# All key-value products of an attention, MLP and expert kernel made early and parked in DRAM, and the last chunk's routing drawn into three steps

## Chip, cores and metric

One Trainium2 chip, one of its cores. The metric is the device time of one execution in microseconds (us). Three runs of the kernel before gave a median of 1302.85 us (1300.02 to 1303.67).

## What is computed

Three stages follow each other on 4608 tokens (8 batches of 576), with 512 features each.

```python
kv = np.einsum('bhsd,bhse->bhde', k, v)          # 8 x 8 heads, 64 x 64 each
out = np.einsum('bhsd,bhde->bhse', q, kv)
rms = np.sqrt(np.mean(out * out, axis=-1, keepdims=True) + 1e-06)
x = out / rms * g_norm                           # then (4608, 512)
h = x @ w_in                                     # 512 -> 2048
x = (h * np.clip(h + 3.0, 0.0, 6.0) / 6.0) @ w_out
do_compute = x @ w_skip > 0                      # routing
e_idx = np.argmax(x[do_compute] @ w_gate, axis=1)
y[mask] = gate_w[mask, None] * (np.maximum(xc[mask] @ w1[e], 0.0) @ w2[e])
```

Only the tokens that pass the skip test go through one of 8 experts (512 -> 1024 -> 512); the others are copied.

## The kernel before

**Products of keys and values.** Two heads at a time make a pair; 8 batches times 4 pairs give 32 products `K(j)`, each a 128x128 sum over 576 positions (five matmuls, the last over 64 rows). A product is masked to its two diagonal blocks (`K2m`, DVE), and split into a high part (`K2h`, ACT) and a low part (`K2`, DVE) so that reduced-precision matmuls can be summed to full precision. `load_kv` (L298), `st_K` (L337) and `st_K2` (L355) do this. Products 0 to 7 are loaded whole into weight buffers that are still empty (`WX[0]`). Products 8 to 31 go through one small buffer with token `kv`: first three of the five pieces (`load`, L306), the matmuls on them (`Ka`), then the other two pieces into the same buffer (`load2`, L315 and L316), and their matmuls (`K`). `Ka` is held until the first chunk's results have left (`("y", 1, 1)`).

**Attention.** Tokens come in 16 units of 288 (`u`), four head pairs each. `st_A` multiplies queries by the product, `st_B` sums the squares, `st_N` and `st_X` normalise and split the result into the high and low parts `xh`, `xl`.

**First MLP.** `convert` (L637) brings in 32 pieces of `w_in` and `w_out`, which lie in memory as 64-bit numbers, through the 4 buffers `SG`; each takes four or five DVE instructions of 128x512 (L661, L665, L668, L672, L676), some of them put on POOL, then a high part on ACT (L679) and a low part (L682). Pieces 24 to 31 land in weight slots 6 and 7. The tokens go through in 13 chunks, 3 of 256 and 10 of 384; `G1` is the first layer of one slice of 128 hidden features (L726), `G1e` its activation and split (`t`, `gh`, `gl`; L762, L767, L771, L778), `G2` the second layer (L717). The low part `gl` has two buffers in this stage.

**Order.** All of this is handed to a planner (`Plan`): each operation has an engine, a cost, dependencies and tokens (`TOKENS`, numbers of buffers), and a priority made of its longest path to the end and an entry of the table `BIAS`. The planner writes each engine's instructions in a fixed order. SP issues nearly all transfers, in such an order too.

**Routing and experts.** Each finished 128-token tile is written to DRAM (`y_scr` and the output), scored (`rt_dot`), and its token numbers are scattered into a table by expert (`rt_scatter`, L921, on POOL). For the last chunk's three tiles this happens inside the first expert's `block`: ten steps, in which step f gives the first layer of slice f, and from step 2 on the second layer of slice f-2, and a list `sd[f]` of side work. There `rt_pe` transposes a tile (L843), `rt_pe2` multiplies it by the routing weights (L852), `rt_pick` and `rt_exp` choose the expert, `rt_rank` (L901, L902) and `rt_slot` number the tokens; then the index lists are loaded (`ix_load`, L960), the tokens' rows gathered from `y_scr` (`f_load`, L966) and transposed for the same block's second half (`f_T`, L978), in steps 8 and 9. The expert weights come in through `w_load` (L617).

Of the kernel before, what the change touches and what calls it, by code (L numbers as in the profile page):

```python
# [31 lines left out]
    "h": 2, "y": 3, "oA": 1, "oB": 1, "oy": 1, "km": 1, "kh": 4, "kl": 4, "kv": 1, "q": 1, "qs": 2, "ss": 2, "a": 3,  # L32
    "t": 1, "g": 3, "gl": 2, "row": 4, "rt": 2,
}
BIAS = {
# [17 lines left out]
    ("ql", 4): 242, ("rank", 0): 171, ("rank", 1): 276, ("scat", 0): 210, ("scat", 1): -1, ("slot", 0): -202,  # L53
    ("slot", 1): 92, ("y", 0): -66, ("y", 1): 246, ("yd", 0): 167, ("yd", 1): -270, "bo": 4, "bump": -174,
    "bump2": -17, "consts": -99, "cp": -169, "cs": -186, "cs1": -132, "fT": -311, "fTh": -228, "fTl": 28,
    "g": -29, "ixc": -190, "late h": -166, "late l": 17, "rowsc": 153, "swap": 74, "tab": -8, "tok": -232,
    "w": -113, "w9": -82, "wh": -60, "wl": -7, "wlo": 183, "z": 75, "zero": -249,
# [4 lines left out]
class Plan:  # L62
# [15 lines left out]
    def kind(name):  # L78
# [7 lines left out]
        if k in ("kv", "kvb", "K", "Ka", "K2", "K2m", "K2h"):  # L86
            return (k, min(n // 4, 2) + (n >= 12))
# [122 lines left out]
def fused_kernel(ctx, tc, qT, kvm, kvr, gv, w_in, w_out, w9, w9t, w1, w2, cst, tokid, out):  # L210
# [7 lines left out]
    dram = ctx.enter_context(tc.tile_pool(name="dram", bufs=1, space=bass.MemoryType.DRAM))  # L218
    y_scr = dram.tile([NTOK, DM], F32, name="y_scr")
# [6 lines left out]
    GL = gpool.tile([128, 2 * 384], F32R, bufs=1, name="gl")  # L226
    gl_free = [0, 1]
    gl_n = [0]

    def gl_next():  # L230
        gl_n[0] += 1
        a = gl_n[0] % 3 * CH
        return GL[:, a:a + CH]

# [63 lines left out]
    def load_kv(j):  # L298
        b, p = divmod(j, 4)

        def load(_):
            if j < 8:
                t = WX[0][j % 4].rearrange("p a b -> p (a b)")[:, 0:1280].rearrange("p (a b c) -> p a b c", a=2, b=5)
            else:
                kv_t[j] = apool.tile([128, 2, 3, 128], F32, tag="kv", name="kv")
                nc.sync.dma_start(kv_t[j], kvm[b, p][:, :, 0:3, :])  # L306
                return
            kv_t[j] = t
            nc.sync.dma_start(t[:, :, 0:4, :], kvm[b, p])
            nc.sync.dma_start(t[0:64, :, 4, :], kvr[b, p])  # L310

        def load2(_):
            t = apool.tile([128, 2, 3, 128], F32, tag="kv", name="kv")
            kv_t[j] = t
            nc.sync.dma_start(t[:, :, 0:1, :], kvm[b, p][:, :, 3:4, :])  # L315
            nc.sync.dma_start(t[0:64, :, 1, :], kvr[b, p])  # L316
# [19 lines left out]
    def st_K(j):  # L336
        def mm(_):  # L337
            t = kv_t.pop(j)
            if j < 4:
                ps = ps_h.tile([128, 128], F32, tag="h", name="kvp")  # L340
            else:
                ps = ps_o.tile([128, 128], F32, tag="o", name="kvp") if j not in kvp_t else kvp_t[j]
            a = 0 if j < 8 or j not in kvp_t else 3
            for i in range(a, 3 if j >= 8 and not a else 5):
                n = 128 if i < 4 else 64
                nc.tensor.matmul(ps, t[0:n, 0, i - a, :], t[0:n, 1, i - a, :], start=(i == 0), stop=(i == 4))  # L346
            kvp_t[j] = ps
# [64 lines left out]
    k_tok = lambda j: "h" if j < 4 else "oB" if j < 8 else "oy"  # L412
# [225 lines left out]
    def convert(n, key, i):  # L638
# [49 lines left out]
        if s >= 4:  # L688
            war += [("K", s), ("K", s - 4)]
# [6 lines left out]
        if s >= 6:  # L696
            war += [("X", 2, p) for p in range(4)]
# [631 lines left out]
```

## Time and profile before

| | us |
|---|---|
| median of 3 runs | 1302.85 |
| the profiled execution | 1304.07 |
| its span, first to last instruction | 1302.1 |
| PE (TensorE) busy | 1244.7 (96%) |
| DVE (VectorE) busy | 882.6 (68%) |
| ACT (ScalarE) busy | 569.1 (44%) |
| POOL (GpSimd) busy | 426.9 (33%) |
| mean granted TensorE clock | 0.983 |

The busy share of PE is a mean over stages: while the weights come in (0 to 160 us) it is far lower than in the long stage behind (240 to 970 us). A row of a view by stretches gives the stretch, its length, each engine's busy time with the number of instructions, the granted TensorE clock as a share of full speed, the share of time in which the DMA engines were busy and the rate in GB/s. The matmuls on full 32-bit operands show as two records each.

### The profile page before, as it was taken

What the parts mean: (1) busy time and instruction counts of PE and PEld (TensorE: products, weight loads), DVE (VectorE), ACT (ScalarE), POOL (GpSimd) and SP (SyncE); (2) the same over time, 40 slices, a digit from 0 to 9 for tenths busy, and PEclk for the clock granted to TensorE, in tenths of its full rate; (3) what the DMA queues carried; (4) which work ended last, traced back from release to release, by engine and by line L of the source; (5) the groups of instructions that cost most, each with busy time, mean ns of one, the idle gap of its engine ahead of it and who ended that gap; (6) DMA issues with size and microseconds to landing.
All of it is one profiled execution on the core that took longest, in us unless ns stands there. A gap on an engine that the chain in (4) does not pass through costs nothing.

```text
span 1302.1 us, 19968 instructions
## 1 busy us (share of the span) xinstructions
PE 1244.7 (96%) x6909; PEld 1108.0 (85%) x6909; DVE 882.6 (68%) x2238; ACT 569.1 (44%) x1345; POOL 426.9 (33%) x409
## 2 busy tenths in 40 slices
PE   5788999999999999999999999999997999999998
PEld 3567898989898998989989898989886888889887
DVE  6999978967769385866838586684855265555342
ACT  2454455545354453525435462543343254444231
POOL 3667633422323142312404342340433122122201
PEclk9689999999999999999999999999998999999999
DMA  9343251213022021202111220101255165555220
GB/s 324 125 94 101 96 181 50 66 51 99 6 73 72 10 81 46 85 1 81 47 28 58 69 68 6 63 1 49 82 162 136 37 192 164 172 185 156 88 70 33
DMA packets 84148, 114.31 MB, mean 88 GB/s; under 512 B 17542, under 2 KB 51222, under 8 KB 83888
## 3 DMA queue, kind: packets, MB, share of 16 engines
q1 hardware_dynamic: 77472, 98.12, 24.8%
q0 software_dynamic: 6544, 14.58, 3.4%
q8 instruction: 64, 1.05, 0.4%
q14 instruction: 68, 0.56, 0.2%
HBM read 91.25 MB, written 26.05 MB: 90 GB/s over the span
## 4 chain that ended last, share of the span: by engine, by line
PE 77%; DMA 9%; DVE 7%; issue 4%; POOL 1%; POOLq 1%; ACT 1%; SPq 0%; DVEq 0%; ACTq 0%
PE y L717 34%; PE h L726 33%; DMA rows<-y_scr,idx 6%; PE kvp L346 3%; PE h L717 2%; DVE wbits L665 1%; DVE wbits L661 1%; DVE SG L672 1%; PE xp L978 1%; DMA kv<-kvr 1%; DMA sh<-kvm 1%; DVE SG L668 1%; POOLq L1058 1%; DMA tab<-pay,slot 1%; PE m L481 1%
## 5 line engine op out<-in xcount | busy, mean ns | idle before, releaser
L834 DVE CUSTOM_DVE_ANT_0 junk<-ysb,w9b 128x512 bf16<-128x512 f32 x297 | 245.5, 827 | 7.2 <-ACT ysb L813 4.5
L762 ACT ACTIVATE t<-h,half 128x384 f32<-128x384 f32 (+1 forms) x208 | 115.6, 556 | 254.5 <-POOL gl L778 126.0
L778 POOL TENSOR_TENSOR gl<-t,gh 128x384 fp32r<-128x384 f32 (+1 forms) x111 | 122.5, 1104 | 272.2 <-PE y L717 175.3
L771 ACT ACTIVATE gh<-t 128x384 fp32r<-128x384 f32 (+1 forms) x208 | 103.0, 497 | 103.9 <-DVE t L767 90.2
L767 DVE SCALAR_TENSOR_TENSOR t<-t,h 128x384 f32<-128x384 f32 (+1 forms) x208 | 107.4, 519 | 53.9 <-ACT t L762 52.6
L717 PE MATMUL y<-wh,gh 128*128 128x512 f32 x400 | 123.5, 400 | 0.0
L726 PE MATMUL h<-xh,wh 128*128 128x384 f32 (+1 forms) x608 | 117.9, 316 | 5.0 <-DVE t L767 2.9
L778 DVE TENSOR_TENSOR gl<-t,gh 128x384 fp32r<-128x384 f32 (+1 forms) x97 | 65.1, 672 | 84.3 <-PE y L717 54.1
L717 PE MATMUL y<-wl,gh 128*128 128x512 f32 x400 | 120.2, 391 | 0.1
L717 PE MATMUL y<-wh,gl 128*128 128x512 f32 x400 | 120.2, 391 | 0.0
L717 PE MATMUL y<-WH,gh 128*128 128x512 f32 x384 | 120.1, 405 | 0.0
L717 PE MATMUL y<-WL,gh 128*128 128x512 f32 x384 | 115.7, 394 | 1.5 <-POOL WL L682 1.4
L717 PE MATMUL y<-WH,gl 128*128 128x512 f32 x384 | 115.3, 393 | 0.0
L726 PE MATMUL h<-xh,wl 128*128 128x384 f32 (+1 forms) x608 | 115.1, 311 | 0.0
L726 PE MATMUL h<-xl,wh 128*128 128x384 f32 (+1 forms) x608 | 114.7, 310 | 0.0
L726 PE MATMUL h<-xh,WH 128*128 128x384 f32 (+1 forms) x496 | 106.6, 331 | 7.1 <-DVE t L767 4.1
L726 PEld LDWEIGHTS h<-xh,wh 128*128 128x128 f32 x608 | 97.9, 189 | 15.6 <-DVE t L767 5.2
L726 PE MATMUL h<-xh,WL 128*128 128x384 f32 (+1 forms) x496 | 102.1, 322 | 0.0
L726 PE MATMUL h<-xl,WH 128*128 128x384 f32 (+1 forms) x496 | 101.0, 319 | 0.0
L726 PEld LDWEIGHTS h<-xh,WH 128*128 128x128 f32 x496 | 85.1, 194 | 18.7 <-DVE t L767 8.0
L1033 DVE SCALAR_TENSOR_TENSOR gl<-h,gh 128x256 fp32r<-128x256 f32 x88 | 37.2, 423 | 91.7 <-ACT gh L1032 80.3
L726 PEld LDWEIGHTS h<-xh,wl 128*128 128x128 f32 x608 | 97.2, 189 | 0.0
(182 smaller groups left out, 2422.9 us busy)
## 6 DMA issues: line engine op xcount, KB each, us to landing
stg<-w SPq DMA_DIRECT2D x64, 512.0 KB
kv<-kvm SPq DMA_DIRECT2D x24, 384.0 KB
y_scr<-ysb SPq DMA_DIRECT2D x36, 256.0 KB
final<-ysb SPq DMA_DIRECT2D x36, 256.0 KB
SG<-w_in SPq DMA_DIRECT2D x16, 512.0 KB
SG<-w_out SPq DMA_DIRECT2D x16, 512.0 KB
q<-qT SPq DMA_DIRECT2D x52, 144.0 KB
sh<-kvm SPq DMA_DIRECT2D x8, 512.0 KB
```

Source lines behind the costliest of these rows:

```text
L346: nc.tensor.matmul(ps, t[0:n, 0, i - a, :], t[0:n, 1, i - a, :], start=(i == 0), stop=(i == 4))
L481: nc.tensor.matmul(m, boR, sl, start=False, stop=True)
L661: nc.vector.tensor_scalar(conv[n], H, 3, 0x3FFFFFF8, op0=ALU.logical_shift_left, op1=ALU.bitwise_and)
L665: nc.vector.scalar_tensor_tensor(t, H, -(1 << 30), t, op0=ALU.bitwise_and, op1=ALU.bitwise_or)
L717: nc.tensor.matmul(ps, st[a], mv[b], start=first and (a, b) == (0, 0) and all(p[0] is not ps for p in prods[:q]), stop=last and (a, b) == ...
L726: nc.tensor.matmul(ps, st[a], mv[b], start=first and (a, b) == (0, 0) and all(p[0] is not ps for p in prods[:q]), stop=last and (a, b) == ...
L762: nc.scalar.activation(t, h_t[c, f], ACTF.Relu, bias=half, scale=1.0 / 6.0)
L767: nc.vector.scalar_tensor_tensor(t, t, 1.0, h_t.pop((c, f)), op0=ALU.min, op1=ALU.mult)
L771: nc.scalar.activation(gh, g_t[c, f], ACTF.Copy)
L778: eng_of[e].tensor_tensor(gl, t, f32(gh), op=ALU.subtract)
L834: nc.vector.tensor_tensor_reduce(junk, ysb[i], W9["t"][:, j, :], 1.0, 0.0, ALU.mult, ALU.add, accum_out=lg[:, j:j + 1])
L1033: nc.vector.scalar_tensor_tensor(gl, ps, 0.0, f32(gh), op0=ALU.max, op1=ALU.subtract)
```

## The change

Products 8 to 31 are now loaded whole, into two of the empty weight buffers in turn, and made as soon as their data is there. Each is copied unmasked out of PSUM by ACT (`Kc`) and written to a DRAM buffer of its own (`Kd`); when its turn comes it is fetched (`Km`), masked by DVE and split as before. The conversions into slots 6 and 7 wait for the last products. The buffer `kv` goes; `gl` gets a third buffer. `t` moves to another pool, and in the last chunk takes a `row` buffer (4 of them). In the first expert block the routing of the last chunk takes steps 0 to 2 instead of 0 to 3, the index loads and gathers step 3 instead of 4, the reading of the counts step 4 instead of 5. The transposed tiles `yT` lie in the second expert's row buffers. The table `BIAS` has other numbers throughout, so the planner's order differs everywhere in the first stage.

```diff
     def load_kv(j):
         b, p = divmod(j, 4)
 
+        n = j % 4 if j < 8 else 2 + j % 2
+
         def load(_):
-            if j < 8:
-                t = WX[0][j % 4].rearrange("p a b -> p (a b)")[:, 0:1280].rearrange("p (a b c) -> p a b c", a=2, b=5)
-            else:
-                kv_t[j] = apool.tile([128, 2, 3, 128], F32, tag="kv", name="kv")
-                nc.sync.dma_start(kv_t[j], kvm[b, p][:, :, 0:3, :])
-                return
+            t = WX[0][n].rearrange("p a b -> p (a b)")[:, 0:1280].rearrange("p (a b c) -> p a b c", a=2, b=5)
             kv_t[j] = t
             nc.sync.dma_start(t[:, :, 0:4, :], kvm[b, p])
             nc.sync.dma_start(t[0:64, :, 4, :], kvr[b, p])
 
-        def load2(_):
...
-        d = [] if j < 4 else [("K", j - 4)] if j < 8 else [("kvb" if j > 8 else "kv", j - 1)]
-        op(("kv", j), "S", 1.24 if j < 8 else 0.45, load, d, dma=1.64 if j < 8 else 1.1, take=["kv"] if j >= 8 else [])
-        if j >= 8:
-            op(("kvb", j), "S", 1.24, load2, [("Ka", j)], dma=0.6, take=["kv"])
+        d = [] if j < 4 else [("K", j - 4 if j < 8 else j - 2)]
+        op(("kv", j), "S", 1.24, load, d, dma=1.64)
...
-        if j < 8:
-            op(("K", j), "PE", 2.1 if j < 3 else 1.12, mm, [("kv", j)], take=[k_tok(j)])
-        else:
-            op(("Ka", j), "PE", 0.67, mm, [("kv", j), ("y", 1, 1)], take=[k_tok(j), "km", "kh", "kl"], give=["kv"])
-            op(("K", j), "PE", 0.45, mm, [("kvb", j)], give=["kv"])
+        op(("K", j), "PE", 2.1 if j < 3 else 1.12, mm, [("kv", j)], take=[k_tok(j)])
...
+        def keep(_):
+
+            kvs_t[j] = WX[1][2][:, j % 4, 300:428]
+            nc.scalar.activation(kvs_t[j], kvp_t.pop(j), ACTF.Copy)
+
+        def fetch(_):
+            kvs_t[j] = apool.tile([128, 128], F32, tag="km", name="km")
+            nc.sync.dma_start(kvs_t[j], k_scr[j])
+
+        def mask(_):
+            nc.vector.tensor_tensor(kvs_t[j], kvs_t[j], bo, op=ALU.mult)
...
+        if j < 8:
+            op(("K2m", j), "V", 0.2, km1, [("K", j)], take=["km"], give=[k_tok(j)])
+        else:
+            op(("Kc", j), "A", 0.25, keep, [("K", j)] + [("Kd", j - 4)] * (j >= 12), give=[k_tok(j)])
+            op(("Kd", j), "S", 0.45, lambda _: nc.sync.dma_start(k_scr[j], kvs_t[j]), [("Kc", j)], dma=0.2)
+            op(("Km", j), "S", 0.45, fetch, [("Kd", j)] + [("Km", j - 1)] * (j > 8), take=["km"], dma=0.2)
+            op(("K2m", j), "V", 0.2, mask, [("Km", j)])
+        op(("K2h", j), "A", 0.2, high, [("K2m", j)], take=["kh"])
+        op(("K2", j), "V", 0.2, low, [("K2h", j)], take=["kl"], give=["km"])
...
-    k_tok = lambda j: "h" if j < 4 else "oB" if j < 8 else "oy"
+    k_tok = lambda j: "h" if j < 4 else "oB"
...
         if s >= 4:
-            war += [("K", s), ("K", s - 4)]
+            war += [("K", s), ("K", s - 4)] + [("K", s + 24)] * (s >= 6)
...
+        if s == 6:
+            war += [("Kd", j) for j in range(28, 32)]
...
-            sd[0] += each(rt_pe, ls[0:2])
-            sd[1] += each(rt_pe, ls[2:]) + each(rt_pe2, ls[0:2]) + each(rt_pick, ls[0:2]) + each(rt_exp, ls[0:2])
-            sd[2] += each(rt_pe2, ls[2:]) + each(rt_rank, ls[0:1]) + each(rt_pick, ls[2:]) + each(rt_exp, ls[2:])
-            sd[3] += each(rt_rank, ls[1:]) + each(rt_slot) + [rt_count] + each(rt_scatter)
-            sd[4] += [lambda: ix_load(idx[0], 256, 2, 2, nc.gpsimd), lambda: ix_load(idx[1], EST, 4, 0, nc.gpsimd)]
-            sd[4] += [lambda: f_load(sets[0], 2, t0=2), lambda: f_load(sets[1], 4)]
-            sd[5] += [lambda: begin(0), lambda: announce(0)]
+            sd[0] += each(rt_pe)
+            sd[1] += each(rt_pe2) + each(rt_pick) + each(rt_exp)
+            sd[2] += each(rt_rank) + each(rt_slot) + [rt_count] + each(rt_scatter)
+            sd[3] += [lambda: ix_load(idx[0], 256, 2, 2, nc.gpsimd), lambda: ix_load(idx[1], EST, 4, 0, nc.gpsimd)]
+            sd[3] += [lambda: f_load(sets[0], 2, t0=2), lambda: f_load(sets[1], 4)]
+            sd[4] += [lambda: begin(0), lambda: announce(0)]
```

**Order on PE, weight stage.** `kvp<-sh` is one whole product from a weight buffer, `o<-q` the attention's products, `h<-x` the first layer, `y<-` the second. Before, the seventh and eighth product stand here, and they are the last whole ones:

```order
L346 MATMUL kvp<-sh_107 128x128 x5
L436 MATMUL o<-qh,kh 128x288
L437 MATMUL o<-qh,kl 128x288
L438 MATMUL o<-ql,kh 128x288
L717 MATMUL y<-WH,gh 128x512 x2
L717 MATMUL y<-WL,gh 128x512 x2
L717 MATMUL y<-WH,gl 128x512 x2
L478 MATMUL m<-sl_111,boR 128x288
L346 MATMUL kvp<-sh_108 128x128 x5
```

With the change, at nearly the same count of rows, the thirteenth and fourteenth:

```order
L329 MATMUL kvp<-sh_138 128x128 x5
L433 MATMUL o<-qh,kh 128x288
L434 MATMUL o<-qh,kl 128x288
L435 MATMUL o<-ql,kh 128x288
L716 MATMUL y<-WH,gh 128x512 x2
L716 MATMUL y<-WL,gh 128x512 x2
L716 MATMUL y<-WH,gl 128x512 x2
L329 MATMUL kvp<-sh_139 128x128 x5
```

Before, products 8 to 31 stand in 48 further rows (24 of three matmuls, 24 of two), the first behind 38 first-layer slices, the last behind 160. Now all 32 stand ahead of the 25th slice: 16 ahead of the seventh, 28 ahead of the twentieth. At the 34th slice both orders hold the same 408 first-layer and 168 second-layer matmuls, with 8 products before and 32 now. Up to the last weight piece's conversion DVE has 261 instructions before and 264 now, of nearly the same kinds.

**Order on SP, weight stage** (`SG` are weight pieces, `sh` and `kv` keys and values, `q` and `sl` queries). Before:

```order
L698 DMA SG<-w_in 128x4x256
L330 DMA sl_109<-qT 128x288 x4
L698 DMA SG<-w_out 128x1024 x2
L306 DMA kv<-kvm 128x2x384
L698 DMA SG<-w_in 128x4x256
L330 DMA q<-qT 128x288
L698 DMA SG<-w_out 128x1024
L698 DMA SG<-w_in 128x4x256 x5
```

With the change:

```order
L697 DMA SG<-w_out 128x1024
L301 DMA sh_138<-kvm 128x2x512
L302 DMA sh_138<-kvr 64x2x128
L376 DMA k_scr_68<-sl_142 128x128
L352 DMA km<-k_scr_66 128x128
L301 DMA sh_139<-kvm 128x2x512
L302 DMA sh_139<-kvr 64x2x128
L376 DMA k_scr_69<-sl_142 128x128
L697 DMA SG<-w_in 128x4x256 x2
```

Between the weight pieces there now stand key-value loads, each of which waits for the product two before it, and stores, each of which waits for its copy. One fetch stands among them; the other 23 stand behind row 120, in the next stage.

**Order on PE, first expert block.** Before, behind the second layer of slice 0 (step 2):

```order
L717 MATMUL y<-WH,gl 128x512 x2
L852 MATMUL lgp<-W9T,yT 128x9 x4
L901 LDWEIGHTS triu
L901 MATMUL pr<-oh,triu 128x8
L902 LDWEIGHTS ones
L902 MATMUL pr<-acc,ones 128x8
L726 MATMUL h<-xh,WH 128x256 x2
```

With the change, at the same place:

```order
L716 MATMUL y<-WH,gl 128x512 x2
L899 LDWEIGHTS triu
L899 MATMUL pr<-oh,triu 128x8
L900 LDWEIGHTS ones
L900 MATMUL pr<-acc,ones 128x8
L899 LDWEIGHTS triu
L899 MATMUL pr<-oh,triu 128x8
```

All three ranks (`pr`) and the count stand here now, and the third tile's routing product (`lgp`) has gone ahead into step 1; before, two ranks and the count came a step later.

## Rows read from the trace of the kernel before

**Rows 1.** The page: engines' busy time, and the chain that ended last.

```profile
PE 1244.7 (96%) x6909; PEld 1108.0 (85%) x6909; DVE 882.6 (68%) x2238; ACT 569.1 (44%) x1345; POOL 426.9 (33%) x409
...
PE 77%; DMA 9%; DVE 7%; issue 4%; POOL 1%; POOLq 1%; ACT 1%; SPq 0%; DVEq 0%; ACTq 0%
```

**Rows 2.** Busy time by stretches, columns as named in the section on time.

```profile
core 0: us, PE busy (x) PEld busy (x) DVE busy (x) ACT busy (x) POOL busy (x), PEclk, DMA share, GB/s
0.00:10.00 10.00, 0.00 (x0) 0.00 (x0) 5.12 (x13) 1.92 (x2) 3.50 (x8) 1.00 0.76 255
10.00:40.00 30.00, 23.23 (x72) 16.71 (x72) 24.20 (x44) 11.26 (x27) 12.23 (x8) 0.89 1.03 341
40.00:80.00 40.00, 26.79 (x129) 21.92 (x128) 36.81 (x69) 19.65 (x54) 25.88 (x24) 0.76 0.29 85
80.00:120.00 40.00, 36.38 (x213) 30.88 (x212) 39.01 (x60) 20.55 (x50) 30.13 (x25) 0.94 0.38 94
120.00:160.00 40.00, 36.80 (x227) 31.31 (x226) 40.00 (x58) 16.48 (x36) 26.09 (x21) 1.00 0.32 104
240.00:970.00 730.00, 726.92 (x3823) 653.76 (x3821) 511.37 (x1466) 333.54 (x791) 226.15 (x228) 1.00 0.19 56
```

**Rows 3.** Timeline, first expert block: routing, gather, first use; idle before in brackets.

```profile
976.83 0.17 PE L902 MATMUL pr<-acc,ones 128*128 128x8 bf16 x1
...
979.73 0.18 PE L901 MATMUL pr<-oh,triu 128*128 128x8 bf16 x1
...
980.67 1.01 POOL L921 DMA_INDIRECT tab<-pay,slot  x1 [23.96 <-DVE sm L913]
...
983.91 6.46 SPq L617 DMA_DIRECT2D stg<-w  x3
...
991.19 1.61 POOL L960 DMA_DIRECT2D idx<-tab  x2 [6.45 <-DMA tab<-pay,slot]
...
1000.40 1.11 PE L978 MATMUL xp<-ident,rows 128*128 128x128 f32 x4 [7.76 <-DMA rows<-y_scr,idx]
```

**Rows 4.** Timeline of PE around two parts of one product: start, length, instruction.

```profile
301.36 0.83 PE L346 MATMUL kvp<-kv 128*128 128x128 f32 x6
301.94 0.95 PE L717 MATMUL y<-wh,gh 128*128 128x512 f32 x3
...
306.56 0.80 PE L346 MATMUL kvp<-kv 128*128 128x128 f32 x4
307.29 0.98 PE L726 MATMUL h<-xh,WH 128*128 128x384 f32 x4
```

**Rows 5.** Line L346: records, ns least/median/most, first and last start.

```profile
L346 PE MATMUL kvp<-kv x240: 270/275/377, 183.4 to 757.8; 128*128 128x128 f32 x96, 64*128 64x128 f32 x24
L346 PE MATMUL kvp<-sh x80: 272/421/582, 10.0 to 74.5; 128*128 128x128 f32 x64, 64*128 64x128 f32 x16
```

**Rows 6.** PE's waits over the whole span: total us, times, longest.

```profile
PE kvp L346 <- DMA kv<-kvm: 1.0, 2, 0.6
PE kvp L346 <- DMA kv<-kvr: 0.9, 2, 0.7
```

**Rows 7.** Lines of the same kind as the added ones, and SP's issues, as in rows 5.

```profile
L363 DVE TENSOR_TENSOR km<-kvp,boR x28: 277/291/293, 56.0 to 758.1; 128x128 f32<-128x128 f32 x28
L369 ACT ACTIVATE kh<-km x28: 295/311/328, 56.4 to 759.0; 128x128 fp32r<-128x128 f32 x28
L306 SPq DMA_DIRECT2D kv<-kvm x24: 542/543/835, 35.0 to 745.1; - x24
L1154 SPq DMA_DIRECT2D tab<-sl x5: 361/480/1765, 79.8 to 82.7; - x5
```

**Rows 8.** The chain that ended last, 501 us: start, us, what.

```profile
501.10 0.54 SPq L315
501.64 0.05 issue
501.69 4.19 DMA kv<-kvr
```

**Rows 9.** By stretches, around that wait, columns as in rows 2.

```profile
995.00:1000.00 5.00, 0.00 (x0) 0.00 (x0) 0.18 (x1) 0.00 (x0) 3.13 (x3) 0.62 0.88 285
1000.00:1005.00 5.00, 4.53 (x14) 3.44 (x14) 1.95 (x4) 1.73 (x5) 3.02 (x3) 0.50 0.52 148
```

**Rows 10.** Timeline of ACT: a high part of the last quarter of the weights.

```profile
140.90 0.63 ACT L679 ACTIVATE wh<-wbits 128x512 fp32r<-128x512 f32 x1 [0.24 <-DVE wbits L676]
```

More of the change, by code (lines that the diff above doesn't have):

```diff
@@ L31 @@
 TOKENS = {
-    "h": 2, "y": 3, "oA": 1, "oB": 1, "oy": 1, "km": 1, "kh": 4, "kl": 4, "kv": 1, "q": 1, "qs": 2, "ss": 2, "a": 3,
-    "t": 1, "g": 3, "gl": 2, "row": 4, "rt": 2,
+    "h": 2, "y": 3, "oA": 1, "oB": 1, "oy": 1, "km": 1, "kh": 4, "kl": 4, "q": 1, "qs": 2, "ss": 2, "a": 3,
+    "t": 1, "g": 3, "gl": 3, "row": 4, "rt": 2,
 }
 BIAS = {
[17 rows of a table removed]
[L53 to L57, printed above, removed]
[10 rows of a table added]
+    ("cl", 7): -252, ("dot", 0): -138, ("dot", 1): 140, ("exp", 0): 188, ("exp", 1): -86, ("g", 1): 48,
[6 rows of a table added]
+    ("ql", 3): -93, ("ql", 4): -52, ("rank", 0): 285, ("rank", 1): 185, ("scat", 0): 246, ("scat", 1): -166,
+    ("slot", 0): -206, ("slot", 1): -231, ("y", 0): 15, ("y", 1): 196, ("yd", 0): 162, ("yd", 1): 178, "bo": -207,
+    "bump": -139, "bump2": 50, "consts": 93, "cp": -52, "cs": -141, "cs1": 38, "fT": -195, "fTh": -188,
+    "fTl": 101, "g": -19, "ixc": -70, "late h": -209, "late l": -183, "rowsc": 68, "swap": 106, "tab": 134,
+    "tok": 234, "w": -230, "w9": -188, "wh": -138, "wl": 144, "wlo": -255, "z": -119, "zero": 202,
 }
@@ L85, in kind @@
             return ("cl" if name[2] in ("sg", "l") else "c", n // 4)
-        if k in ("kv", "kvb", "K", "Ka", "K2", "K2m", "K2h"):
+        if k in ("kv", "K", "Kc", "Kd", "Km", "K2", "K2m", "K2h"):
             return (k, min(n // 4, 2) + (n >= 12))
@@ L102, in alone @@
         if eng == "VP":
+            return True
+        if name[0] == "K2m" and name[1] >= 8:
             return True
@@ L218, in fused_kernel @@
     dram = ctx.enter_context(tc.tile_pool(name="dram", bufs=1, space=bass.MemoryType.DRAM))
+    k_scr = [dram.tile([128, 128], F32, name=f"k_scr{j}") for j in range(32)]
     y_scr = dram.tile([NTOK, DM], F32, name="y_scr")
@@ L225, in fused_kernel @@
     rpool = ctx.enter_context(tc.tile_pool(name="rpool", bufs=4))
[L226 to L233, printed above, removed]
     spool = ctx.enter_context(tc.tile_pool(name="spool", bufs=3))
@@ L341, in mm @@
             else:
-                ps = ps_o.tile([128, 128], F32, tag="o", name="kvp") if j not in kvp_t else kvp_t[j]
-            a = 0 if j < 8 or j not in kvp_t else 3
-            for i in range(a, 3 if j >= 8 and not a else 5):
+                ps = ps_o.tile([128, 128], F32, tag="o", name="kvp")
+            for i in range(5):
                 n = 128 if i < 4 else 64
-                nc.tensor.matmul(ps, t[0:n, 0, i - a, :], t[0:n, 1, i - a, :], start=(i == 0), stop=(i == 4))
+                nc.tensor.matmul(ps, t[0:n, 0, i, :], t[0:n, 1, i, :], start=(i == 0), stop=(i == 4))
             kvp_t[j] = ps
-        if j < 8:
-            op(("K", j), "PE", 2.1 if j < 3 else 1.12, mm, [("kv", j)], take=[k_tok(j)])
-        else:
-            op(("Ka", j), "PE", 0.67, mm, [("kv", j), ("y", 1, 1)], take=[k_tok(j), "km", "kh", "kl"], give=["kv"])
-            op(("K", j), "PE", 0.45, mm, [("kvb", j)], give=["kv"])
+        op(("K", j), "PE", 2.1 if j < 3 else 1.12, mm, [("kv", j)], take=[k_tok(j)])
     def st_K2(j):
@@ L380, in st_K2 @@
             return
-        op(("K2m", j), "V", 0.2, km1, [("K", j)], take=["km"] if j < 8 else [], give=[k_tok(j)])
-        op(("K2h", j), "A", 0.2, high, [("K2m", j)], take=["kh"] if j < 8 else [])
-        op(("K2", j), "V", 0.2, low, [("K2h", j)], take=["kl"] if j < 8 else [], give=["km"])
+        if j < 8:
[7 more added lines that the diff above has]
+        op(("K2", j), "V", 0.2, low, [("K2h", j)], take=["kl"], give=["km"])
     def st_q(u, p):
@@ L750, in G1 @@
         op(("G1", c, f), "PE", 1.44 if c < 3 else 2.09, mm, deps, take=["h"], bonus=1.28)
-    h_t, gl_at = {}, {}
+    h_t = {}
     def G1e(c, f):
@@ L760, in relu @@
             else:
-                t = gpool.tile([128, 384], F32, tag="t", bufs=1, name="t")[:, 0:CW[c]]
+                at, tag, n = (rpool, "row", 4) if stg else (apool, "t", 1)
+                t = at.tile([128, 384], F32, tag=tag, bufs=n, name="t")[:, 0:CW[c]]
             nc.scalar.activation(t, h_t[c, f], ACTF.Relu, bias=half, scale=1.0 / 6.0)
@@ L775, in low @@
             t, gh = g_t[c, f]
-            gl_at[c, f] = gl_free.pop(0)
-            gl = GL[:, gl_at[c, f] * 384:gl_at[c, f] * 384 + CW[c]]
+            gl = gpool.tile([128, 384], F32R, tag="gl", name="gl")[:, 0:CW[c]]
             eng_of[e].tensor_tensor(gl, t, f32(gh), op=ALU.subtract)
@@ L790, in mm @@
             gh, gl = g_t.pop((c, f))
-            gl_free.append(gl_at[c, f])
             wh, wl = wt["out", f // 4]
@@ L843, in rt_pe @@
             nc.tensor.transpose(ps[:, k, :], ysb[i][:, k * 128:(k + 1) * 128], ident)
-        t = rpool.tile([128, 4, 128], F32, tag="row", name="yT")
+        t = sets[1][2][i - LT].rearrange("p (k c) -> p k c", k=4)
         nc.scalar.activation(t, ps, ACTF.Copy)
@@ L1030, in g1 @@
             gh = gpool.tile([128, CH], F32R, tag="gh", name="gh")
-            gl = gl_next()
+            gl = gpool.tile([128, 384], F32R, tag="gl", name="gl")[:, 0:CH]
             nc.scalar.activation(gh, ps, ACTF.Relu)
@@ L1089, in tr @@
                 gh = gpool.tile([128, 2, 128], F32R, tag="gh", name="gh")
-                gl = gl_next().rearrange("p (a c) -> p a c", a=2)
+                gl = gpool.tile([128, 384], F32R, tag="gl", name="gl")[:, 0:CH].rearrange("p (a c) -> p a c", a=2)
                 nc.scalar.activation(gh, ps[:, 2 * a:2 * a + 2, :], ACTF.Copy)
```

4 lines of the change are left out of this document (removed), and 33 rows, old and new, of the table BIAS.

## The prediction

> **What bounds the kernel now.** The page first: PE is busy 96% of the span and holds 77% of the chain that ended last [rows 1]. So only what takes work or waits off PE counts, and a mean over stages can't tell where. The view by stretches can [rows 2]. From 240 to 970 us PE is busy 726.92 of 730 us at full clock: there every matmul taken out is time gained. Ahead of 160 us it is different. PE is busy 23.23 of 30, then 26.79, 36.38 and 36.80 of 40 us, with the granted clock at 0.89, 0.76, 0.94 and 1.00. DVE is busy 36.81, 39.01 and 40.00 of 40 us in the same stretches: it turns the weights into high and low parts, and PE can't run ahead of them. So the kernel has a weight stage that DVE sets, with room on PE, and a long stage that PE sets, with none. The last chunk's routing is a third place: PE waits 7.76 us for gathered rows [rows 3].
>
> **Products out of the long stage.** A product's first part takes 0.58 us from its start to the start of the next instruction, its second 0.73 us [rows 4]; they recur 24 times, 240 records between 183 and 758 us [rows 5]. 24 x 1.31 = 31.4 us. PE's waits for their loads add 1.0 and 0.9 us [rows 6]. Together 33.3 us leave the long stage.
>
> **Products into the weight stage.** The same 31.4 us are added there. What room is there, from 10 us, when PE starts? Idle: 6.8 + 13.2 + 3.6 + 3.2 = 26.8 us [rows 2]. Time lost to the clock: 23.23 x 0.11 + 26.79 x 0.24 + 36.38 x 0.06 = 11.2 us. In all 38.0 us. Not all can be filled, since PE waits for DVE in between: in 120 to 160 us, with DVE busy throughout, PE still stood idle 8% of the time, and I take that share for what stays of the 150 us, 12.0 us. So 26.0 us are filled, and 31.4 - 26.0 = 5.4 us push the stage's end back. The bounds: nothing, if DVE's work alone sets the end (DVE's own list is as long as before), and 31.4 us, if none fits. The row of 120 to 160 us is the nearest, since DVE and PE are both loaded there as they will be.
>
> The clock is in this sum as regained. The rows show 0.76 where PE was busy 26.79 of 40 us, 0.94 at 36.38 and 1.00 at 36.80 [rows 2]. The Trainium skill, page "TensorE: Matmul & The Clock Gate", section on the clock gate, says that the lower rate is the default state and that activity releases it; by that all 11.2 us come back, and the sum is the one above. The row of 80 to 120 us speaks against a full return, as it fell once more there; by the row without any return the stage ends 16.6 us later instead of 5.4 (the first rival).
>
> **What else the parking adds.** 24 copies on ACT: 0.31 us each by the nearest copy [rows 7], 7 us among 90 us in which ACT is about half busy; hidden, since other rows of PE stand between most products. 24 masks on DVE, as before, at 0.29 us. On SP two loads of 0.54 us and a store of 0.48 us for each product [rows 7]: 24 x 1.6 = 38 us of issue between about 25 and 110 us, beside weight pieces; hidden while SP isn't held (the second rival). 24 fetches in the long stage, 0.48 us of issue each, in place of three load issues each; fewer than before. From fetch to split product it is at most 0.5 + 4.2 + 3 x 0.3 = 5.6 us, taking the landing of a key-value load [rows 8] for the far smaller fetch; the four buffers of the split products cover it, since all four are made before the unit that uses them. If that cover is gone PE waits (the third rival). Other bound: nothing. I take nothing. The third buffer of `gl`, the place of `t` and the new table of priorities act in the long stage, where PE has 3.1 us idle in 730 [rows 2]: at most that gained, and up to as much again lost; I take nothing.
>
> **Routing.** The second and third rank and the count move from behind step 3's products to behind step 2's: in the trace 979.73 against 976.83 us, 2.9 us [rows 3]. But the three tiles' choices on DVE now come in one row ahead of the ranks, so PE may wait there; I take half, 1.4 us, by which the scatter, the index load, the gather and the end of the 7.76 us wait come earlier. PE's own work ahead of the wait is the same, so what it waits for the ranks is taken from the later wait. Bounds: nothing; and the whole 7.76 us, if the scatter now gets ahead of the expert weight loads (issued from 983.91 us, ahead of its landing, which POOL waited 6.45 us for). Then the clock would not fall either: it was at 0.62 in the wait and at 0.50 behind it, with 4.53 us busy [rows 9], of which half, 2.3 us, would come back. The steps behind keep their work.
>
> **The sum.** 33.3 - 5.4 + 1.4 = 29.3 us off the profiled execution's 1304.07 us, 1274.8 us. That execution lay 1.2 us above the median of the runs, 1302.85 us, so against the median I give 1274 us.
>
> **Rivals.**
>
> First, the weight stage fills worse: the clock stays as it was. The room is then 26.8 - 12.0 = 14.8 us, 16.6 us push the end back, and the gain is 33.3 - 16.6 + 1.4 = 18.1 us: 1285 us. For it: the first products ran at a median of 421 ns a record, against 275 later [rows 5], and new products come into just that stretch. Against: they fill the gaps in which it fell. Chance 0.13.
>
> Second, and slower than before: SP starves the weight stage. Each store stands in SP's queue until its copy is done, and the next loads and weight pieces stand behind it. A load takes 1.1 us of issue and 4.2 us to land [rows 8], its product 1.3 us: 6.6 us a round, and with two buffers 3.3 us a product. From about 26 us the 24 products then end at 105 us, and the last quarter of the weights, which must wait for them, is written from 140.9 us on [rows 10]: 36 us to spare. If the held queue lets only one buffer run at a time, the pace is 6.6 us, the last product comes at 184 us, 43 us late, and the kernel gets 43 - 34.7 = 8 us slower: 1311 us. It decides from 6.2 us a product. The Trainium skill, page "DMA: Bandwidth & Descriptors", section "Anatomy of one DMA", says that a wait for a semaphore takes place on the issuing sequencer, ahead of the dispatch; by that rule the holding is certain, and only its length is open. Against it: each store stands right behind a load that has waited for the same product, so it adds no more than the copy's wait; and the DMA engines are busy only 0.29 to 0.38 of the time from 40 us on [rows 2]. Chance 0.05.
>
> Third, the fetches come late: one of each group of four finds no cover, 6 x 5.6 = 33.6 us of waits in the long stage, which takes back the whole gain: 1302 us, no change. Against it: such waits took only 1.9 us in the kernel before, with larger loads and one buffer [rows 6]. Chance 0.05.
>
> That the products don't move is out: the order shows all of them ahead of the 25th slice.
>
> **How the numbers follow.** The forecast has a chance of 0.77, the rivals 0.13, 0.05 and 0.05. The low end: all products fit (33.3) and the routing's wait goes whole with its clock (7.8 + 2.3): 43.4 us, 1260 us. The high end: the first rival with nothing from the routing and 1 us of new waits, 1287 us. That range leaves out the second and third rivals, and some tails. Faster by over 0.3% (3.9 us, about what a measurement of this kernel can tell from no change) holds in the forecast and the first rival: 0.90. Within 0.3% is the third, 0.05, slower the second, 0.05.
>
> **What would show it.** Right: no product behind 160 us; the long stage with PE as busy as before and ended some 28 us earlier; PE busy over 90% and at a clock near 1 from 40 to 120 us; DVE as busy there as before; the wait for gathered rows near 6 us. Wrong: DVE idle in the weight stage for weight pieces (second rival), a clock of 0.8 from 40 to 80 us (first), PE's waits for a split product or a fetch over 5 us in the long stage (third).

## The result: 1268.9 us, and the profile after

The changed kernel took 1268.91 us (median of 4 runs, 1267.16 to 1275.1) against 1303.26 us on the same chip: a ratio of 0.9748, 95% interval 0.9709 to 0.9787. A second set of 5 runs gave 1267.07 us, ratio 0.9723 (0.9706 to 0.9740). The forecast was 1274 us, 1260 to 1287. The profiled execution took 1270.19 us, its span 1268.4 us, 33.7 us under the one before.

The page, answering to [rows 1], engines' busy time:

```profile
PE 1231.2 (97%) x6909; PEld 1103.5 (87%) x6909; DVE 873.0 (69%) x2216; ACT 574.6 (45%) x1369; POOL 436.9 (34%) x431
```

Busy time by stretches, answering to [rows 2]:

```profile
10.00:40.00 30.00, 22.73 (x106) 17.31 (x106) 27.55 (x57) 14.84 (x42) 13.18 (x14) 0.94 1.03 350
40.00:80.00 40.00, 38.81 (x238) 34.56 (x239) 35.61 (x60) 19.00 (x52) 23.38 (x20) 0.87 0.77 234
80.00:120.00 40.00, 38.67 (x239) 33.46 (x237) 30.98 (x48) 20.89 (x57) 25.29 (x25) 1.00 0.71 197
120.00:160.00 40.00, 39.99 (x253) 34.96 (x252) 34.98 (x53) 15.21 (x37) 25.21 (x21) 1.00 0.73 228
240.00:935.00 695.00, 693.67 (x3602) 627.15 (x3600) 508.57 (x1468) 335.33 (x792) 235.77 (x239) 1.00 0.13 42
```

From 40 to 120 us PE is now busy 77.48 of 80 us, before 63.17. DVE, which was hardly free there, is now idle up to a quarter of the time (30.98 of 40 us). The weight stage has changed its bound from DVE to PE. DMA is busy 0.71 to 0.77 of the time, before 0.29 to 0.38.

The products' line answers to [rows 5]; records, ns least, median, most, first and last start:

```profile
L329 PE MATMUL kvp<-sh x320: 270/275/582, 12.5 to 148.1; 128*128 128x128 f32 x128, 64*128 64x128 f32 x32
```

All 320 records lie ahead of 149 us, where 240 lay between 183 and 758.

PE's longest waits, then DVE's between 10 and 180 us (what waited, for what; total us, times, longest):

```profile
PE kvp L329 <- DMA sh<-kvm: 13.6, 2, 12.5
PE kvp L329 <- DVE sl L535: 4.8, 2, 2.5
PE xp L976 <- DMA rows<-y_scr,idx: 4.6, 1, 4.6
```

```profile
DVE wbits L658 <- DMA SG<-w_in: 5.7, 1, 5.7
DVE t L767 <- ACT t L762: 5.1, 7, 2.0
```

The first product's load lands at 12.5 us, before at 10.0. SP's timeline shows what goes ahead of it (start, length, what):

```profile
3.73 0.43 SPq L314 DMA_DIRECT2D sl<-qT  x1
4.21 0.91 SPq L697 DMA_DIRECT2D SG<-w_out  x2
6.07 0.67 SPq L301 DMA_DIRECT2D sh<-kvm  x1
```

A load of queries and two weight pieces go ahead of it; before, the first key-value load went out at 3.64 us.

**Four marks** in PE's records divide the span: the last matmul of the 34th first-layer slice (by then the kernels have made the same matmuls, but for the products), the first matmul of the first expert block, the first use of gathered rows (`xp`, [rows 3]), and the last matmul. Starts in us, each from the start of its own trace. In the last three rows the second layer stands elsewhere at the first mark, 6 records ahead, 6 behind and 12 behind, at 0.23 us each.

| run | 34th slice | block | `xp` | last |
|---|---|---|---|---|
| before | 171.37 | 967.08 | 1000.40 | 1296.14 |
| changed | 177.09 | 935.58 | 967.05 | 1262.25 |
| changed, second trace | 178.40 | 937.42 | 966.95 | 1259.69 |
| changed, old routing | 179.62 | 938.95 | 972.55 | 1267.37 |
| before, new routing | 169.79 | 966.31 | 995.30 | 1288.46 |
| changed, products twice | 209.44 | 968.39 | 998.31 | 1292.06 |
| before, products twice | 169.88 | 999.59 | 1033.48 | 1329.34 |
| changed, two fifths | 174.32 | 933.23 | 963.80 | 1281.20 |
| before, two fifths | 170.91 | 955.52 | 990.20 | 1309.53 |
| changed, stores and fetches twice | 232.43 | 1007.43 | 1035.49 | 1328.84 |
| changed, spare stores | 177.14 | 937.34 | 969.03 | 1263.98 |
| changed, plan for two `gl` | 178.61 | 969.29 | 998.52 | 1293.10 |
| changed, old table | 242.50 | 1029.06 | 1056.49 | 1350.45 |
| changed, old table, two `gl` | 242.50 | 1034.96 | 1062.19 | 1357.72 |

So the weight stage ends 5.7 us later (7.0 in the second trace), the long stage (34th slice to block) takes 758.49 instead of 795.72 us, 37.2 less, and from block to `xp` it is 31.47 instead of 33.32 us.

### The profile page after: what moved, and what is told of

The parts are those of the page before. It is cut to its first block, busy times and chain, and to the rows that moved or that the text cites. A ratio compares the mean times of both kernels' runs of the same rounds, so it can differ in the third digit from the quotient of the medians.

```text
span 1268.4 us, 20136 instructions
## 1 busy us (share of the span) xinstructions
PE 1231.2 (97%) x6909; PEld 1103.5 (87%) x6909; DVE 873.0 (69%) x2216; ACT 574.6 (45%) x1369; POOL 436.9 (34%) x431
## 5 line engine op out<-in xcount | busy, mean ns | idle before, releaser
L777 POOL TENSOR_TENSOR gl<-t,gh 128x384 fp32r<-128x384 f32 (+1 forms) x130 | 136.4, 1050 | 252.5 <-ACT gh L771 151.5
L725 PE MATMUL h<-xh,WH 128*128 128x384 f32 (+1 forms) x496 | 103.3, 324 | 2.8 <-ACT xh L989 1.6
L1030 ACT ACTIVATE gh<-h 128x256 fp32r<-128x256 f32 x88 | 33.9, 385 | 145.2 <-PE h L725 140.0
L1007 POOL DMA_INDIRECT final<-rows,idx x26 | 26.2, 1009 | 204.7 <-DVE rows L1006 201.7
```

What stands on the lines that cost most here:

```text
L725: nc.tensor.matmul(ps, st[a], mv[b], start=first and (a, b) == (0, 0) and all(p[0] is not ps for p in prods[:q]), stop=last and (a, b) == ...
L777: eng_of[e].tensor_tensor(gl, t, f32(gh), op=ALU.subtract)
L1007: inst = nc.gpsimd.indirect_dma_start(out=out[:, :], out_offset=bass.IndirectOffsetOnAxis(ap=ix[:, t, 0:1], axis=0), in_=o, in_offset=None ...
L1030: nc.scalar.activation(gh, ps, ACTF.Relu)
```

## The experiments

**What a product's matmuls are worth in either place.** Products 8 to 31 made twice, in the changed kernel and in the kernel before:

```diff
-            for i in range(5):
+            for i in list(range(5)) * (2 if j >= 8 else 1):
```

```diff
-            for i in range(a, 3 if j >= 8 and not a else 5):
+            r = list(range(a, 3 if j >= 8 and not a else 5)) * (2 if j >= 8 else 1)
+            for m, i in enumerate(r):
...
-                nc.tensor.matmul(ps, t[0:n, 0, i - a, :], t[0:n, 1, i - a, :], start=(i == 0), stop=(i == 4))
+                nc.tensor.matmul(ps, t[0:n, 0, i - a, :], t[0:n, 1, i - a, :], start=(i == 0 and m == 0), stop=(i == 4 and m == len(r) - 1))
```

> The changed kernel, with the matmuls of products 8 to 31 made twice over; the second pass starts the sums again, so the output stays. It adds 240 records, 26.9 us at 0.112 us or 31.4 us at 0.131 us, to the weight stage. Theory, that the room of the weight stage is used up (26 us filled, 5.6 us spilled): nearly all comes on top, +22 to +31 us, 1291 to 1300 us. Rival, that room is left and the 5.6 us delay has another cause (the later first key load, stores on SP's queue): under +10 us.

> The kernel before, with the matmuls of products 8 to 31 made twice over within the same pieces (the sums double and the normalised result stays, within rounding). It adds 240 records to the long stage. Theory: their full time, +26.9 to +31.4 us, about 1330 to 1335 us. Rival, that part of a piece's time is a fixed switching cost and the clock gives some back: +20 us or less.

The changed kernel took 1301.84 us (ratio to the kernel before 0.9983, 0.9965 to 1.0), the other 1336.15 us (1.0257, 1.0240 to 1.0274). In the kernel before, the long stage grew from 795.72 to 829.71 us, 34.0 us or 1.42 us a product. In the changed kernel the 34th slice came 32.4 us later than in its first trace, 31.0 later than in its second, and the long stage stayed (758.94 us). Both cost a little more than expected; the rivals fall. No room is left in the weight stage. Its stretch with the products doubled:

```profile
80.00:120.00 40.00, 40.00 (x261) 35.24 (x261) 22.44 (x38) 15.57 (x41) 20.39 (x19) 1.00 0.62 170
```

PE is never idle, and DVE falls to 22.44 of 40 us. The stage takes up one set of products, at the price of the 5.7 to 7.0 us by which its end moved, and has no room for a second.

**Fewer matmuls.** Only two of the five pairs of matmuls of products 8 to 31:

```diff
-            for i in range(5):
+            for i in range(5) if j < 8 else (0, 4):
```

```diff
-            for i in range(a, 3 if j >= 8 and not a else 5):
+            for i in range(a, 5) if j < 8 else ((4,) if a else (0,)):
```

> The changed kernel, of whose products 8 to 31 only two of the five pairs of matmuls are made (the sums over three fifths of the tokens are left out). It takes 24 x 6 = 144 matmul records from the weight stage, 16.1 to 18.9 us of TensorE time (at 0.112 us a record, the pieces' slope, or 1.31 us / 10). Theory, that the weight stage had 26 us of room and the products spilled over it by 5.6 us (34th slice at 176.95 instead of 171.37 us): no more than those 5.6 us can come back, so 0 to -5.6 us against the changed kernel, some 1265 us. Rival, that TensorE now sets the weight stage from end to end: -16 to -19 us, some 1251 us.

> The kernel before, of whose products 8 to 31 only two of the five pairs of matmuls are made (three fifths of the tokens are left out of these sums); both pieces of a product stay where they are, with their loads. The same 144 matmul records are taken from the long stage, where TensorE is busy all the time. Theory: the whole of their time comes off the end, -16 to -19 us, 1285 to 1287 us. Rival, that the pieces cost the long stage mainly their waits and switching and not their matmuls: well under 10 us.

(The first expectation's 176.95 us, counted from another zero, is 177.09 here.) 1288.15 us (0.9887, 0.9871 to 0.9904) and 1316.94 us (1.0114, 1.0097 to 1.0131). These totals don't stand against the full kernels: with other sums other tokens pass the routing, and the experts' line `gl<-h,gh` runs 96 times instead of 88. The marks ahead of the experts do. In the changed kernel the 34th slice comes 2.8 us earlier (174.32), 4.1 against the second trace: inside the expected 0 to 5.6. It is still 3.0 us behind the kernel before, so matmuls are not all that pushed the stage back. The later first load, which starts PE 2.5 us later and stays in this run, can be another cause, and so can the key-value loads, for which PE waits 5.3 us here (five times, 40 to 200 us); no run took either away. In the kernel before only 11.1 us leave the long stage, not 16 to 19. Its waits tell a part of it (171 to 955 us; in [rows 6] 0.9 us for `kvr` and 1.0 for `kvm`):

```profile
PE kvp L346 <- DMA kv<-kvr: 4.1, 5, 1.5
PE kvp L346 <- DMA kv<-kvm: 0.6, 2, 0.3
```

With one small buffer the next part is not there so soon: part of what the matmuls took had covered loads. These waits are 2.8 us more than before; the other 2 us or more of the shortfall stay open.

**The routing alone.** The four-step lists put back into the changed kernel, and the three-step lists put into the kernel before, with the buffer of `yT` each time:

```diff
-            sd[0] += each(rt_pe)
-            sd[1] += each(rt_pe2) + each(rt_pick) + each(rt_exp)
-            sd[2] += each(rt_rank) + each(rt_slot) + [rt_count] + each(rt_scatter)
...
+            sd[0] += each(rt_pe, ls[0:2])
...
+            sd[3] += each(rt_rank, ls[1:]) + each(rt_slot) + [rt_count] + each(rt_scatter)
```

> The changed kernel, with the four-step routing of the last chunk and its buffer as in the kernel before. Theory: the table of the second expert block reaches DRAM 1.4 us later after the block's start and the wait for the gathered rows grows from 4.6 us to about 6.5 us, +1.4 to +2.1 us, about 1270.7 us. Rival, that the three-step routing only moves work and the gather ends when its queue lets it: within 0.4 us of the changed kernel.

> The kernel before, with the three-step routing of the last chunk alone (transposes in the second expert's row buffers, as in the changed kernel). Theory: -1.4 to -2.1 us, about 1301.5 us, with the wait for the gathered rows near 5.5 us instead of 7.76 us. Rival, that the earlier scatter only makes the wait start sooner or that the extra VectorE work of a step delays a slice: 0 or slower.

1276.4 us (0.9790, 0.9774 to 0.9806) and 1296.66 us (0.9950, 0.9932 to 0.9968). Both theory and rival were too small. The routing is worth 0.0050 of 1303 us, 6.5 us (4.2 to 8.9), in the kernel before. In the changed one it is 0.0067, 8.7 us, to its second set, and 0.0042, 5.5 us, to its first, whose interval is wide. The timeline of the kernel before with the new routing answers to [rows 3]:

```profile
978.71 1.02 POOL L921 DMA_INDIRECT tab<-pay,slot  x1 [22.87 <-DVE sm L913]
...
981.34 0.98 POOL L921 DMA_INDIRECT tab<-pay,slot  x1 [0.30 <-issue]
985.55 1.61 POOL L960 DMA_DIRECT2D idx<-tab  x2 [3.23 <-DMA tab<-pay,slot]
986.47 4.19 SPq L617 DMA_DIRECT2D stg<-w  x3
...
995.30 0.66 PE L978 MATMUL xp<-ident,rows 128*128 128x128 f32 x4 [1.80 <-DMA rows<-y_scr,idx]
```

The first of the three scatters comes 1.2 us earlier after the block's start (12.40 against 13.59 us), but POOL's wait for the landing of the last (the arrival of its data) also shrinks from 6.45 to 3.23 us. In the kernel before the last scatter starts here:

```profile
983.30 1.44 POOL L921 DMA_INDIRECT tab<-pay,slot  x1 [0.30 <-issue]
```

There the expert weight loads go out 0.6 us behind its start [rows 3]; with the new routing they go out behind the index load. The changed kernel with the old routing shows the former once more:

```profile
955.17 1.44 POOL L919 DMA_INDIRECT tab<-pay,slot  x1 [0.30 <-issue]
955.79 6.33 SPq L614 DMA_DIRECT2D stg<-w  x3
962.86 1.61 POOL L958 DMA_DIRECT2D idx<-tab  x2 [6.25 <-DMA tab<-pay,slot]
...
972.55 1.12 PE L976 MATMUL xp<-ident,rows 128*128 128x128 f32 x4 [8.05 <-DMA rows<-y_scr,idx]
```

The first trace of the changed kernel lies between: the weight loads go out at 954.66 us, the index load at 956.14, the landing took 4.85 us and PE's wait 4.6. The second trace has the index load first:

```profile
952.83 0.98 POOL L919 DMA_INDIRECT tab<-pay,slot  x1 [0.30 <-issue]
956.72 1.60 POOL L958 DMA_DIRECT2D idx<-tab  x2 [2.91 <-DMA tab<-pay,slot]
957.16 4.81 SPq L614 DMA_DIRECT2D stg<-w  x3
```

PE then waits 2.16 us. So the size differs between executions, and goes with which of the two is issued first. All 14 traces agree. In the four with the four-step lists the weight loads go out 16.8 us after the block's start and the landing takes 6.25 to 7.78 us. In the ten with the three-step lists they go out after 19.1 to 21.1 us and the landing takes 2.72 to 3.45 us, or 4.85 in the two in which they still go out ahead of the index load. So the new routing does not only bring the scatter forward; it also puts the weight loads, which wait for DVE in SP's queue, back by 2 to 4 us. No run moved the weight loads alone, so that they lengthen the landing is not shown apart.

The rest comes behind `xp`. About 8 us from `xp` on, in the changed kernel with the old routing, then in its first and in its second trace (columns as in [rows 2]):

```profile
972.44:976.44 4.00, 3.89 (x12) 3.21 (x13) 1.96 (x4) 1.70 (x4) 2.89 (x3) 0.50 0.64 172
976.44:980.44 4.00, 3.52 (x29) 3.28 (x28) 2.40 (x5) 1.05 (x3) 1.04 (x1) 0.97 0.49 137
```

```profile
966.91:970.91 4.00, 3.86 (x12) 3.10 (x13) 1.96 (x4) 1.70 (x4) 2.01 (x2) 0.50 0.72 275
970.91:974.91 4.00, 3.53 (x27) 3.13 (x26) 2.43 (x5) 1.04 (x3) 0.91 (x1) 0.84 0.53 141
```

```profile
966.98:970.98 4.00, 3.53 (x22) 2.98 (x23) 2.64 (x7) 2.36 (x6) 1.76 (x2) 1.00 1.02 361
970.98:974.98 4.00, 4.00 (x33) 3.91 (x32) 2.04 (x4) 1.15 (x3) 2.04 (x2) 1.00 0.95 295
```

After 8.05 us of idle PE the clock is 0.50 for the next 4 us, and after the 4.6 us of the first trace it is as low; after 2.16 us it stays at 1.00: 12 records in the first 4 us against 22. From `xp` to the last matmul it is 294.82, 295.20 and 292.74 us. So the changed kernel gets the clock back in its second trace and not in its first.

**Parking.** Every store and fetch of a parked product issued twice; then only the stores, the second one to a place of its own:

```diff
             nc.sync.dma_start(kvs_t[j], k_scr[j])
+            nc.sync.dma_start(kvs_t[j], k_scr[j])
...
-            op(("Kd", j), "S", 0.45, lambda _: nc.sync.dma_start(k_scr[j], kvs_t[j]), [("Kc", j)], dma=0.2)
+            op(("Kd", j), "S", 0.45, lambda _: [nc.sync.dma_start(k_scr[j], kvs_t[j]) for _ in range(2)], [("Kc", j)], dma=0.2)
```

```diff
+    k_two = [dram.tile([128, 128], F32, name=f"k_two{j}") for j in range(32)]
...
-            op(("Kd", j), "S", 0.45, lambda _: nc.sync.dma_start(k_scr[j], kvs_t[j]), [("Kc", j)], dma=0.2)
+            op(("Kd", j), "S", 0.45, lambda _: [nc.sync.dma_start(x[j], kvs_t[j]) for x in (k_scr, k_two)], [("Kc", j)], dma=0.2)
```

> The changed kernel, with each store of a parked product and each fetch of one issued twice (the same data, so the output stays). It adds 24 stores of 32 KB to SP's queue in the weight stage and 24 fetches in the long stage. Theory, that stores and fetches hide: within 1 us. Rival, that SP's queue or the transfers hold up the weights (the 5.7 us wait for w_in that the changed kernel shows before 180 us would grow): +5 us or more.

> The changed kernel, with each product stored a second time to another place in DRAM, which nobody reads; the second store needn't wait for the first to land, as the doubled one did (SP's queue stood 3.4 us for each of 24). Theory, that the 69 us of the doubled stores and fetches are these waits on SP's queue, and the transfers themselves hide: no more than the issue of 24 stores, 24 x 0.5 us = 12 us on SP, of which at most a few reach the end, 1268 to 1274 us. Rival, that any further store starves the weight stage: +20 us or more.

1337.65 us (1.0263, 1.0245 to 1.0281) and 1271.35 us (0.9770, 0.9749 to 0.9791). The first was far off what theory said. (A store is 128x128 numbers of 4 bytes, 64 KB, not the 32 KB of its expectation.) SP's queue with stores and fetches doubled, around one product, and its waits over the span:

```profile
109.51 0.55 SPq L301 DMA_DIRECT2D sh<-kvm  x1
110.15 0.56 SPq L302 DMA_DIRECT2D sh<-kvr  x1
110.80 5.59 SPq L377 DMA_DIRECT2D k_scr<-sl  x2
116.44 0.55 SPq L301 DMA_DIRECT2D sh<-kvm  x1
```

```profile
SPq L377 <- DMA k_scr<-sl: 82.3, 24, 6.0
SPq L353 <- DMA km<-k_scr: 37.9, 23, 3.4
```

In this kernel a second store to the same place is issued only when the first has landed: 82.3 us of standing SP, 3.4 for each of 24. Behind it stand the next loads and weight pieces, and DVE waits for those (10 to 230 us):

```profile
DVE wbits L659 <- DMA SG<-w_out: 23.3, 5, 9.6
DVE wbits L659 <- DMA SG<-w_in: 18.5, 5, 10.2
```

The weight stage ends 55 us later. The long stage takes 16.5 us more; the doubled fetches lie there, and PE's waits grow from 0.9 to 12.7 us, but no run doubled the fetches alone. With a second store that need not wait, the same stored bytes cost 2.4 us (against the first set) to 4.3 us (against the second). So the stores' transfers nearly hide, and the forecast's second rival has a real mechanism: it only needed a store that waits. SP's queue has room for 24 further issues, but not for 82.3 us of standing.

**The plan.** The change also has three buffers for `gl` and other order numbers. Plan for two; then the old table; then both:

```diff
-    "t": 1, "g": 3, "gl": 3, "row": 4, "rt": 2,
+    "t": 1, "g": 3, "gl": 2, "row": 4, "rt": 2,
```

```diff
-    ("A", 0): 50, ("A", 1): -178, ("A", 2): -205, ("A", 3): 78, ("A", 4): 189, ("A2l", 3): 9, ("A2l", 4): 206,
...
+    ("A", 0): 92, ("A", 1): -80, ("A", 2): -123, ("A", 3): 206, ("A", 4): 261, ("A2l", 3): -70, ("A2l", 4): 162,
...
```

> The changed kernel, with the token loads planned for two low-part buffers, as in the kernel before. Theory, that the third buffer's rows came from elsewhere and hold up nothing: within 2 us of the changed kernel. Rival, that the 2 us by which the other gaps of the long stage shrank come from it: +2 us or more.

> The changed kernel with the table of order numbers of the kernel before (operations that are new get none). Theory, that the gain of the long stage needs only the products gone from it, and the table only places them in the weight stage: up to +12 us, 1269 to 1281 us, all of it ahead of the 34th slice. Rival, that the order has to fit the whole plan, as with the two low-part buffers (1303 us): 1295 us or more, with new waits in the long stage.

> The changed kernel with both the table of order numbers and the two low-part buffers of the plan of the kernel before. Theory, that the 34 us lost with two buffers came from a table made for three: it is no slower than the one with the old table and three buffers, within 6 us of it. Rival, that the two buffers themselves hold up the second layer whatever the order: 20 us or more behind that run.

1302.94 us (1.0001, 0.9988 to 1.0013), 1359.89 us (1.0445, 1.0421 to 1.0469) and 1366.8 us (1.0496, 1.0474 to 1.0519). The first two theories fell; their rivals held, but named no size so large. With the plan for two buffers the weight stage ends about as in the changed kernel (178.61 us), but the long stage takes 790.68 us, 32 more, with no product in it. PE's longest waits from 180 to 969 us, where the changed kernel had under 1 us in all:

```profile
PE m L477 <- ACT sh L455: 10.6, 2, 5.4
PE h L725 <- DVE t L767: 5.6, 2, 5.0
PE h L725 <- ACT xh L569: 3.6, 2, 3.1
```

These are 19.8 of the 32 us; and the granted clock is 0.98 over this span, in the changed kernel 1.00.

With the old table both stages lose: the 34th slice comes at 242.50 us, the long stage takes 786.55 us. In the weight stage one wait stands out (DVE), in this stretch:

```profile
120.00:160.00 40.00, 35.26 (x205) 30.16 (x203) 8.31 (x15) 7.50 (x21) 0.74 (x1) 0.83 0.73 219
```

```profile
175.47 0.69 DVE L679 TENSOR_TENSOR wl<-wbits,wh 128x512 fp32r<-128x512 f32 x1 [35.90 <-DMA k_scr<-sl]
```

The low part that goes into slot 6 must wait for the last parked product's store, which this order issues at 173.0 us instead of 148.7. In the changed kernel no such wait shows. On top of the old table, two buffers instead of three cost 0.0051, 6.6 us; the theory of the last run nearly holds (6.9 us between the medians, 6 expected). That speaks for a table made for another plan, and not the buffer, as the cause of most of the 34 us lost with the new table. It isn't shown: the old table brings waits of its own, which can hide what the buffer costs.

**The changed kernel again.**

> The changed kernel itself, once more, for its median beside the variants and a second trace. Theory, that the routing is worth the 7 us by which the kernel with the old routing and the changed kernel's first runs differ: 1267 to 1271 us. Rival, that the first four runs were low by chance and the routing is worth 2 us, as its stretch of the first trace says: 1273 to 1275 us.

1267.07 us, inside what theory said. That the first set was low by chance is out. No variant beats the changed kernel.

## Why the prediction held

**Products out of the long stage: 33.3 us forecast, 37.2 measured (36.7 in the second trace, 36.4 with the old routing).** The mechanism holds. The term is undersized: the two parts of [rows 4], 1.31 us, are a clean pair, and doubling gave 1.42 us a product. The 48 parts, each counted from the matmul ahead of it to the one behind, with its waits, took some 35 us of the trace before; the remaining 2 us are other gaps between matmuls, fewer now.

**Products into the weight stage: 5.4 us forecast, 5.7 and 7.0 measured (8.3 with the old routing, whose edit leaves that stage alone).** The size is nearly right, the account less so. "PE can't run ahead of them" held only as far as the order of before went: I took it that DVE would stay as busy there and that 8% of PE's time would stay idle behind it. From 80 us on PE is idle 1.3 of 80 us and DVE is the one that waits. What stayed lies ahead of that: 7.3 us idle from 10 to 40 us, 2.5 of it by the later first load, which I had not looked at. The clock came back as taken, to 1.00 from 80 us on, but only to 0.87 from 40 to 80: the first rival would have needed it to stay at 0.76.

The near hit is partly luck. Reckoned as in the forecast, from 10 us on, 9.8 us stayed idle (12.0 taken) and 22.73 x 0.06 + 38.81 x 0.13 = 6.4 us were still lost to the clock (none taken). So 38.0 - 16.2 = 21.8 us of room were filled, not 26.0. But the products took only 27.5 us there (21.8 + 5.7; they are the only matmuls by which the kernels differ up to the mark), not 31.4. Two errors of about 4 us offset each other.

**Routing: 1.4 us forecast, 5.5 to 8.7 measured.** This is the step that failed: "I take half, 1.4 us". I moved the end of the wait by the scatter's shift alone. The scatter does come earlier after the block's start, by 0.8 to 1.5 us (12.78 and 12.10 against 13.59 us in the changed kernel's traces), but its landing also takes 3.2 to 3.5 us less when the weight loads go out behind the index load, and PE's clock stays at 1.00 behind the waits of 1.8 and 2.16 us. That is in part the case of my upper bound, 7.8 + 2.3 us. I had its rows and gave it no weight.

**What else the parking adds: nothing forecast.** Nearly right as to the transfers: 24 spare stores cost 2 to 4 us, and no fetch holds up PE (0.9 us of waits in the whole long stage). The chance of the second rival was right by what the change does, not by how near it lies: its threshold was 6.2 us a product, and with 3.4 us of waiting more for each store, and the fetches doubled, the kernel is 34 us slower than before. The Trainium skill, page "DMA: Bandwidth & Descriptors", section "Anatomy of one DMA", has such a wait take place on the issuing sequencer, ahead of the dispatch; the 82.3 us on SP agree. The third rival's time was added up wrong: 33.6 us against a gain of 29.3 make some 1307 us, not 1302.

**The order: "I take nothing".** The gain forecast was read from the new order, so the table's work was in it unseen. The runs show how much: 91 us with the old numbers, 34 with one buffer count unmatched. My bound, that priorities can lose no more than they can gain in the long stage, was wrong: with the two wrong plans it takes 28 and 32 us more. For the table at hand the bound held, with some 2 us gained.

**In sum** the change without the routing brings 27.4 us (0.0210 of 1303 us, by the run with the old routing; 25.3 to 29.4), against 27.9 forecast. By the medians the 5 us by which the forecast missed, 7 in the second set, are thus the routing. Single traces divide it otherwise. Ahead of the expert block the changed kernel gains 31.5 us in its first trace, 29.7 in its second and 28.1 with the old routing; from there to the last matmul 2.4, 6.8 and 0.6 us. So 27.4 beside 27.9 is in part luck too: a long stage that gained 3 to 4 us more than forecast made up for a weight stage that lost up to 2.9 us more.

**The signs named.** DVE was not as busy in the weight stage as before (30.98 of 40 us against 39.01), and it stood there 5.7 us for a weight piece, which I had named as a sign of the second rival; both came without a loss. The wait for gathered rows was 4.6 and 2.16 us, not near 6.

## What to carry to other kernels

Here work moved nearly for free only into the idle time of its own engine, and only once: doubling the moved work tells how much of that room is left (here none). A transfer that hides is not a queue that may wait: 24 spare stores cost 2 to 4 us, the same stores with 3.4 us of waiting on SP's queue put the weight stage back by 55 us. And where a table of priorities sets the order, a moved operation and its table are one change: with the old numbers the same work was 91 us slower.

## What the runs showed of the hardware

The landing of a small indirect scatter took 6.25 to 7.78 us in four traces where 3 weight loads were issued 0.6 us behind its start, 4.85 us in two where they were issued 4.3 us behind it, and 2.72 to 3.45 us in eight where they followed the index load; that the loads are the cause is not shown apart. After waits of 4.6, 7.76 and 8.05 us TensorE's clock was granted at 0.50, the lower of its two levels (1.2 of 2.4 GHz), in the next 4 us; after waits of 1.8 and 2.16 us it stayed at 1.00. The Trainium skill, page "TensorE: Matmul & The Clock Gate", section on the clock gate, calls the lower rate the default that activity releases; these traces agree.
